# Attention row tiles moved onto multiples of 128, with the last 64 queries of two heads in one tile

## The chip, the cores and the metric

The kernel runs on one core of one Trainium2 chip. The metric is the device time of one execution in microseconds (us), as the median of several runs. A core has TensorE (PE in the profile, its weight loads PEld), VectorE (DVE), ScalarE (ACT), GpSimd (POOL) and SyncE (SP), whose queue issues the DMA transfers.

## What is computed

Three stages follow each other, cut here to what matters:

```
S, D = 576, 64
# 1. causal attention with a cumulative bias, batch 4, 8 heads, head_dim 64
scores = q @ k.T / 8 + min(-(cum[i] - cum[j]), 0)     # masked above the diagonal
x = softmax(scores) @ v
# 2. mixing over the sequence (rank 32), then a feed-forward layer 512 -> 2048 -> 512
u = x + mix(x);  y = u + relu(u @ w_ch1) @ w_ch2
# 3. four attention "experts" (head size 64), each row of y keeps two of four, with gates
out = sum over the two chosen e of w_e * (softmax(q_e @ k_e.T / 8) @ v_e @ wo_e)
```

Both attentions are causal: query row i needs keys 0 to i only. 576 is four times 128 and 64 more.

## The kernel before, in words

**One helper for both attentions.** Class `Attn` serves stage 1 (32 heads, 16 pairs) and stage 3 (16 heads, 8 pairs). A pair is two heads that are worked one after the other; their value products share a PSUM tile. A head's 576 query rows are five row tiles: 64 rows first, then four of 128 that start at 64, 192, 320 and 448. A tile's key width is 64, 192, 320, 448 or 576, since keys beyond the diagonal are left out. A pair is thus ten steps. `run` counts them as `i`, and a step does, in this order of code:

- `qk`: the score products of tile `i` on PE, two matmuls (four for width 576, in two PSUM banks);
- `tr`: the transposes on PE of the tile that is `LAG` steps older (LAG is 10), in blocks of 128 keys, into one of two PSUM tiles `t`. Since tiles end at 64 beyond a multiple of 128, each head also has five tail transposes of 64 keys (line 396) beside its ten of 128 (line 393);
- `peak` (line 363, VectorE): adds the mask, writes the scores to the buffer `P` in SBUF and takes the row maximum;
- `exp` (line 370, ScalarE) of the tile before, in place in `P`, with the row sum;
- `evac` (lines 77 and 79, ScalarE or VectorE as a letter in `ENGA` or `ENGG` says): copies of `t` into the transposed matrix `pt`;
- `norm` (lines 375 to 381), once per head: two small VectorE operations, then GpSimd scales the five tiles of `P`;
- one piece of a value product (`pvq`), then `fillers(i)`.

`P` is two buffers, one for each head of a pair. A tile of `P` is written again ten steps later.

**What fills the steps.** In stage 1 `fillers` takes, per step, pieces of the weight conversion (`convs`: 1 a step, 2 a step between the steps in `FAST`; six pieces convert 128x256 numbers), steps of the operand preparation of the next pair (`PREP`, `PREP1`, `load`), and background work (`BG`: mixing, and the first feed-forward tasks of lines 284 and 298, which wait in the queue until their weight tile is converted). In stage 3 the table `GTAB` names the filler of each step: k and q are query and key products (`g_qk`, line 1064), v values (`g_v`, line 997), a point an output product (`g_out`, line 1087) if one is ready. Stage 2 between them (lines 836 and 854) does not use `Attn`.

**What sets the order.** Stages 1 and 2 run in the order in which the code is written; in stage 3 a scheduler orders each engine's instructions. Each engine works its own queue in order. All DMAs go through SP's queue.

**Operands.** Queries, split into high and low parts, stand in tiles `L1` and `L2`, keys in `R1` and `R2`; the two heads lie side by side. 64 zero columns stand ahead of head 0, so that the first tile can be read as 128 columns. In stage 3 `R1` gets its upper half from `L1` by a DMA, and `L1` then its lower half.

Of the kernel before, what the change touches and what calls it, by code (L numbers as in the profile page):

```python
# [68 lines left out]
TRP = ((1, 0, 2), (2, 2, 3), (3, 3, 4), (4, 0, 0), (0, 4, 5))  # L69
BG = (1, 1, 0, 2, 1)  # L70
# [79 lines left out]
def fused_kernel(ctx, tc, qk, v, s, u, vv, w12, wp, out):  # L150
# [166 lines left out]
    class Attn:  # L317
# [3 lines left out]
        LAG = 10  # L321

        def __init__(self, pools, nq, engines, scale, split=0):
# [4 lines left out]
            self.stat, self.P = [], []  # L328
            for i in range(3):
                t = self.st.tile([P, 3, NT], F32, name=f"stat{i}")  # L330
                nc.vector.memset(t, 1.0)
# [4 lines left out]
            self.pvq = []

        def clear(self, i):


            nc.gpsimd.memset(free_ap(self.pt[i][64:128], 0, [[PST + P, NT], [1, 64]]), 0.0)

        def qk(self, n, t):
            q1, k1, q2, k2 = self.pair_ready(n)
            M, W, i0 = ROWS[t], WID[t], I0[t]
            nb = 1 if W <= 512 else 2
            w = W // nb
            ps = self.psq.tile([P, nb, 512], F32, tag=f"qk{nb}", bufs=1 if nb == 2 else self.nq, name=f"qk_{n}_{t}")
            rows = slice(i0 + M - 64, i0 + M + 64)
            for bk in range(nb):  # L350
                c0 = bk * w
                nc.tensor.matmul(ps[:, bk, :w], lhsT=q1[:, rows], rhs=k1[:, c0:c0 + w], start=True, stop=False)  # L352
                nc.tensor.matmul(ps[:, bk, :w], lhsT=q2[:, rows], rhs=k2[:, c0:c0 + w], start=False, stop=True)  # L353
            return ps[P - M:, :, :w] if nb > 1 else ps[P - M:, 0, :w]
# [11 lines left out]
        def exp(self, n, t):
            M, W = ROWS[t], WID[t]
            stat = self.stat[n % 3]
            po = self.P[n % 2][P - M:, OFF[t]:OFF[t] + W]
            nc.scalar.activation(out=po, in_=po, func=AF.Exp, scale=-1.0, bias=stat[P - M:, 0, t:t + 1],  # L370
                                 accum_out=stat[P - M:, 1, t:t + 1])

        def norm(self, n):
            stat = self.stat[n % 3]
            nc.vector.tensor_scalar(out=stat[:, 2, :], in0=stat[:, 1, :], scalar1=1e-9, scalar2=None, op0=OP.add)
            nc.vector.reciprocal(out=stat[:, 2, :], in_=stat[:, 2, :])  # L376
            gate = self.heads[n].get("gate")
            for t in range(NT):
                r0 = P - ROWS[t]
                pv = self.P[n % 2][r0:, OFF[t]:OFF[t] + WID[t]]  # L380
                nc.gpsimd.tensor_scalar(out=pv, in0=pv, scalar1=stat[r0:, 2, t:t + 1],  # L381
                                        scalar2=1.0 if gate is None else gate(t)[r0:], op0=OP.mult, op1=OP.mult)

        def tr(self, n, r):

            ps = self.pst.tile([P, 512], F32, tag="t", name=f"t_{n}_{r}")
            Pn = self.P[n % 2]
            t, a, e = TRP[r]  # L390
            for kb in range(t):
                c0 = OFF[t] + P * kb
                nc.tensor.transpose(ps[:, P * kb:P * kb + P], Pn[:, c0:c0 + P], ident)  # L393
            for k in range(a, e):
                c0, x = OFF[k] + WID[k] - 64, P * (t + k - a)
                nc.tensor.transpose(ps[0:64, x:x + P], Pn[:, c0:c0 + 64], ident)  # L396
            return ps

        def evac(self, n, r, ps):
            pt = self.pt[n % 3]  # L400
            t, a, e = TRP[r]
            if t:
                cp(nc, self.engines[n % 2][r], free_ap(pt[:, :], I0[t], [[PST, t], [1, P]]), ps[:, :P * t])
            if e > a:
                cp(nc, self.engines[n % 2][r], free_ap(pt[0:64], (PST + P) * a, [[PST + P, e - a], [1, 64]]),
                   free_ap(ps[0:64], P * t + 64, [[P, e - a], [1, 64]]))
# [813 lines left out]
```

## Time and profile before

| what | us |
|---|---|
| median of three runs | 850.0 (849.77 to 850.97) |
| the profiled execution's own time | 849.59 |
| its span, first to last instruction | 847.8 |
| busy in the span | PE 804.4, PEld 743.4, DVE 522.2, ACT 478.3, POOL 329.7 |

The profiled execution stands 1.8 us above its span, and 0.4 us below the median. PE's busy time counts each matmul from its issue to its end; matmuls overlap, so what one costs is read from the distance between the starts of neighbours. The score products of the 24 pairs start at these times: pair 0 at 9.57 us, pair 7 at 115.85, pair 15 (the last of stage 1) at 258.76, pair 16 (the first of stage 3) at 665.45, pair 18 at 699.69, pair 22 at 788.47, pair 23 at 809.74. Stage 2 lies from 295 to 652.

### The profile page before, as it was taken

To read this page: it belongs to the slowest core of one execution; us is meant where nothing else is said; L and a number is where in the kernel's file an instruction comes from. 1 tells how busy PE (TensorE), PEld (TensorE's weight loads), DVE (VectorE), ACT (ScalarE), POOL (GpSimd) and SP (SyncE) were. 2 spreads that over 40 slices of the span, in tenths; PEclk is the share of its full clock that TensorE was granted. 3 is DMA by queue.
4 is the path that set the end of the run, shared out by engine and by line. 5 is a ranking of instruction groups with operands and counts; after the bars stand their busy time and mean duration, and the time that the engine had idled before them with its cause. 6 is when DMAs were issued, how large, how long until landed. Compare 5 with 4: busy or idle time off the path is not lost.

```text
span 847.8 us, 17359 instructions
## 1 busy us (share of the span) xinstructions
PE 804.4 (95%) x6068; PEld 743.4 (88%) x6068; DVE 522.2 (62%) x1547; ACT 478.3 (56%) x1446; POOL 329.7 (39%) x498
## 2 busy tenths in 40 slices
PE   4898799999999999999999999999999989999997
PEld 3676588988888799999999999999999989898875
DVE  7778876786665457646554664464456775656541
ACT  6788777776676445334434443443333576666672
POOL 6656655453453335223422442232333043322241
PEclk9999999999999999999999999999999999999999
DMA  7877566646651151112121221110000221212121
GB/s 212 220 214 208 167 171 187 198 134 169 184 134 44 37 210 51 50 27 55 45 63 26 77 59 42 50 39 26 1 1 2 43 44 29 67 42 54 53 65 62
DMA packets 35897, 75.48 MB, mean 89 GB/s; under 512 B 4584, under 2 KB 8168, under 8 KB 35780
## 3 DMA queue, kind: packets, MB, share of 16 engines
q1 hardware_dynamic: 35812, 74.39, 32.2%
q8 instruction: 48, 0.79, 0.4%
q14 instruction: 37, 0.30, 0.1%
HBM read 38.93 MB, written 8.55 MB: 56 GB/s over the span
## 4 chain that ended last, share of the span: by engine, by line
PE 77%; DVE 5%; ACT 3%; POOL 2%; issue 2%; DMA 0%; SPq 0%; POOLq 0%; DVEq 0%; ACTq 0%
PE hps L836 21%; PE facc L854 21%; PE pv L420 6%; PE qkp L1064 5%; PE t L393 4%; PE facc L298 3%; PE ops L1087 3%; PE hps L284 3%; PE vps L997 3%; PE qk L353 2%; PE qk L352 2%; PE t L396 2%; POOL P L381 2%; DVE P L363 1%; ACT pt L77 1%
## 5 line engine op out<-in xcount | busy, mean ns | idle before, releaser
L268 POOL TENSOR_TENSOR ul<-uT,uh 128x288 fp32r<-128x288 f32 x126 | 101.7, 826 | 172.0 <-ACT uh L267 149.0
L370 ACT ACTIVATE P<-P,stat 64x64 f32<-64x64 f32 (+4 forms) x240 | 133.7, 557 | 44.1 <-DVE stat L363 42.0
L841 DVE SCALAR_TENSOR_TENSOR hl<-hps,hh 128x288 fp32r<-128x288 f32 x110 | 50.4, 458 | 150.0 <-ACT hh L840 150.0
L381 POOL TENSOR_SCALAR P<-P,stat 64x64 f32<-64x64 f32 (+4 forms) x160 | 101.4, 648 | 104.6 <-DVE stat L376 58.1
L363 DVE CUSTOM_DVE_ANT_0 P<-qk,mask 64x64 f32<-64x64 f32 (+4 forms) x240 | 116.4, 487 | 37.6 <-PE qk L353 21.9
L840 ACT ACTIVATE hh<-hps 128x288 fp32r<-128x288 f32 x110 | 45.0, 409 | 147.9 <-PE hps L836 147.6
L77 ACT ACTIVATE pt<-t 64x64 f32<-64x64 f32 (+5 forms) x304 | 89.8, 336 | 41.3 <-PE t L396 35.3
L836 PE MATMUL hps<-uh,wl 128*128 128x288 f32 x376 | 111.2, 296 | 0.0
L836 PE MATMUL hps<-ul,wh 128*128 128x288 f32 x376 | 111.1, 296 | 0.0
L854 PE MATMUL facc<-hh,wh 128*128 128x288 f32 x376 | 111.1, 296 | 0.0
L836 PE MATMUL hps<-uh,wh 128*128 128x288 f32 x376 | 111.0, 295 | 0.0
L854 PE MATMUL facc<-hh,wl 128*128 128x288 f32 x376 | 110.9, 295 | 0.0
L854 PE MATMUL facc<-hl,wh 128*128 128x288 f32 x376 | 110.8, 295 | 0.0
L352 PE MATMUL qk<-R,L 128*128 128x288 f32 (+4 forms) x288 | 94.9, 334 | 16.4 <-DVE L L577 9.6
L393 PE MATMUL t<-ident,P 128*128 128x128 f32 x480 | 88.1, 282 | 11.4 <-ACT pt L77 4.8
L381 POOL TENSOR_SCALAR P<-P,stat,pt 64x64 f32<-64x64 f32 (+4 forms) x80 | 48.5, 620 | 113.1 <-DVE stat L376 57.6
L393 PEld LDWEIGHTS t<-ident,P 128*128 128x128 f32 x480 | 58.8, 142 | 23.3 <-issue 9.4
L352 PEld LDWEIGHTS qk<-R,L 128*128 128x128 f32 x288 | 57.0, 198 | 23.9 <-issue 11.8
L420 PE MATMUL pv<-pt,V 128*64 128x288 f32 (+4 forms) x752 | 76.9, 344 | 0.0
L191 POOL TENSOR_TENSOR wl<-c_a_w,wh 128x256 fp32r<-128x256 f32 x56 | 43.7, 781 | 76.8 <-ACT wh L188 74.2
L836 PEld LDWEIGHTS hps<-uh,wl 128*128 128x128 f32 x376 | 70.9, 189 | 0.0
L854 PEld LDWEIGHTS facc<-hh,wl 128*128 128x128 f32 x376 | 70.9, 188 | 0.0
(186 smaller groups left out, 2145.6 us busy)
## 6 DMA issues: line engine op xcount, KB each, us to landing
c_raw_w<-in_w_dram SPq DMA_DIRECT2D x64, 256.0 KB
uT<-in_qk_dram SPq DMA_DIRECT2D x15, 576.0 KB
L<-HI SPq DMA_DIRECT2D x28, 288.0 KB
V<-in_v_dram SPq DMA_DIRECT2D x16, 320.0 KB
R<-HI SPq DMA_DIRECT2D x14, 288.0 KB
R<-uT SPq DMA_DIRECT2D x14, 288.0 KB
L<-uT SPq DMA_DIRECT2D x14, 288.0 KB
aD<-stage SPq DMA_DIRECT2D x6, 576.0 KB
```

Source lines behind the costliest of these rows:

```text
L77: nc.scalar.activation(out=out, in_=in_, func=AF.Copy)
L268: eng.tensor_tensor(out=l_, in0=src, in1=h_.bitcast(F32), op=OP.subtract)
L352: nc.tensor.matmul(ps[:, bk, :w], lhsT=q1[:, rows], rhs=k1[:, c0:c0 + w], start=True, stop=False)
L363: nc.vector.tensor_tensor_reduce(out=po, in0=view, in1=mk, scale=-self.scale, scalar=3.0e38, op0=OP.add, op1=OP.min, accum_out=stat[P - M: ...
L370: nc.scalar.activation(out=po, in_=po, func=AF.Exp, scale=-1.0, bias=stat[P - M:, 0, t:t + 1], accum_out=stat[P - M:, 1, t:t + 1])
L381: nc.gpsimd.tensor_scalar(out=pv, in0=pv, scalar1=stat[r0:, 2, t:t + 1], scalar2=1.0 if gate is None else gate(t)[r0:], op0=OP.mult, op1=O ...
L393: nc.tensor.transpose(ps[:, P * kb:P * kb + P], Pn[:, c0:c0 + P], ident)
L420: nc.tensor.matmul(out[64 * hh:64 * hh + 64, lo - a:e - a], lhsT=V(hh, kb), rhs=pt[:, PST * kb + lo:PST * kb + e], start=kb == 0, stop=kb ...
L836: nc.tensor.matmul(ps, lhsT=w[:, 0, cs], rhs=x, start=i == 0, stop=i == 11)
L840: nc.scalar.activation(out=hh, in_=ps, func=AF.Relu)
L841: nc.vector.scalar_tensor_tensor(out=hl, in0=ps, scalar=0.0, in1=hh.bitcast(F32), op0=OP.max, op1=OP.subtract)
L854: nc.tensor.matmul(accs[c][d], lhsT=w[:, 1, cs], rhs=x, start=f == fs[0] and i == 0, stop=f == fs[-1] and i == 2)
```

## The change

A head's tiles now start at 0, 128, 256 and 384 with key widths 128, 256, 384 and 512. The last 64 queries of both heads of a pair form a ninth tile of 128 rows and 576 keys. Its scores are a sum: head 0's 64 queries with 64 zero columns behind them, plus 64 zero columns with head 1's 64 queries behind them, eight matmuls into two banks. For that the zeros stand between the heads in `L1` and `L2`, and head 1's queries are rolled by 64 so that its last 64 come first (on the host for stage 1, by split writes and four DMAs in place of two in `g_qk` of stage 3).

A pair is nine steps and `LAG` is 9. `P` is one buffer of nine tiles; a tile is written again nine steps later, in the step in which `tr` reads it. `norm` runs twice a pair, for tiles 0 to 3 at the pair's step 5 and for tiles 4 to 8 at step 1 of the next pair. `tr` of the ninth tile makes five transposes into both PSUM tiles `t`; `evac` makes four copies of them. The mask has a second form for the ninth tile and is built by `Attn`. The gates of stage 3 are placed by a VectorE copy instead of two DMAs. The tables that are counted in steps (`FAST`, `HALVES`, `UFIRST`, `WIDE`, `GTAB`, `BG`, the engines' letters) are written anew.

```diff
-ROWS = [64, 128, 128, 128, 128]
-I0 = [0, 64, 192, 320, 448]
-WID = [64, 192, 320, 448, 576]
+NS = 9
+WID = [128, 256, 384, 512] * 2 + [576]
+OFF = [sum(WID[:s]) for s in range(NS + 1)]
+QB = S + 64
+QA = (0, QB + 64)
-FAST = (40, 70)
+FAST = (36, 63)
-ENGA = ('vaaaaa', 'aavaav')
+ENGA = 'vaaaaavaaavv'
-ENGG = ('aaaava', 'aaaava')
+ENGG = 'aaaaaaaaaavv'
-GTAB = "kkkkvvvvvqqqq......."
+GTAB = "kkkkvvvvvqqqq....."
-BG = (1, 1, 0, 2, 1)
+BG = (2, 1, 1, 0, 2, 1, 1, 1, 1)
...
-        LAG = 10
+        LAG = NS
...
-            for i in range(2):
-                self.P.append(self.st.tile([P, PW], F32, name=f"P{i}"))
-                nc.gpsimd.memset(self.P[i][0:64, 0:64], 0.0)
+            self.P = self.st.tile([P, OFF[NS]], F32, name="P")
...
+        def qk(self, p, s):
+            W = WID[s]
+            if s < NS - 1:
+                h, t = divmod(s, 4)
+                q1, k1, q2, k2 = self.pair_ready(2 * p + h)
+                c0 = QA[h] + P * t
+                ps = self.psq.tile([P, 1, 512], F32, tag="qk1", bufs=self.nq, name=f"qk_{p}_{s}")[:, 0, :W]
+                nc.tensor.matmul(ps, lhsT=q1[:, c0:c0 + P], rhs=k1[:, :W], start=True, stop=False)
+                nc.tensor.matmul(ps, lhsT=q2[:, c0:c0 + P], rhs=k2[:, :W], start=False, stop=True)
+                return ps
+            ps = self.psq.tile([P, 2, 512], F32, tag="qk2", bufs=1, name=f"qk_{p}_{s}")
+            l = [(q[:, 512 + 64 * h:640 + 64 * h], k) for h in range(2)
+                 for q, k in itertools.batched(self.pair_ready(2 * p + h), 2)]
+            for bk in range(2):
+                for x, (q, k) in enumerate(l):
+                    nc.tensor.matmul(ps[:, bk, :HALF], lhsT=q, rhs=k[:, HALF * bk:HALF * bk + HALF],
+                                     start=x == 0, stop=x == 3)
+            return ps[:, :, :HALF]
...
+            for k0 in range(0, WID[s], 512):
+                ps = self.pst.tile([P, 512], F32, tag="t", name=f"t_{p}_{s}_{k0}")
+                for c in range(k0, min(WID[s], k0 + 512), P):
+                    w = min(P, WID[s] - c)
+                    nc.tensor.transpose(ps[0:w, c - k0:c - k0 + P], self.P[:, OFF[s] + c:OFF[s] + c + w], ident)
+                l.append(ps)
...
-                if i % NT == 1 and 1 < i <= n + 1:
-                    self.norm(i // NT - 1)
+                if i % NS == 5 and i < n:
+                    self.norm(i // NS, 0, 4)
+                if i % NS == 1 and 1 < i <= n + 1:
+                    self.norm(i // NS - 1, 4, NS)
...
-            at = 10 * (p - 1)
+            at = NS * (p - 1)
...
             def place():
                 gt = gates[b % 2]
-                nc.sync.dma_start(out=gt[0:64, 1:NT, :], in_=x[64:128, 0:NT - 1, :])
-                nc.sync.dma_start(out=gt[64:128], in_=x[0:64])
+                tt(out=gt, in0=x, in1=wide, op=OP.mult)
+                nc.vector.tensor_copy(out=gt[64:128, NT - 1, 0:E:2], in_=gt[0:64, NT - 1, 1:E:2])
...
             if h == 1 and hf == 1:
                 L1, R1, _ = sets[pr]
-                dma(out=R1[64:128], in_=L1[0:64])
+                dma(out=R1[64:128, 0], in_=L1[0:64, 0])
+                dma(out=R1[64:128, 1, 0:512], in_=L1[0:64, 1, 64:])
+                dma(out=R1[64:128, 1, 512:], in_=L1[0:64, 1, 0:64])
                 dma(out=L1[0:64], in_=L1[64:128])
```

**What moves on PE.** Steps 2 and 3 of pair 7 in stage 1, before (qk_14 is the first head of pair 7, qk_head_tile; t_12 are the transposes of pair 6, mx a mixing task, hps a feed-forward task of twelve matmuls, of which three are shown):

```order
L352 MATMUL qk_14_2_1577<-R1_1_127,L1_1_125 128x320
L353 MATMUL qk_14_2_1577<-HI_1271,L2_1_128 128x320
L393 MATMUL t_12_2_1580<-ident_58,P0_114 128x128 x3
L396 MATMUL t_12_2_1580<-ident_58,P0_114 64x128
L352 MATMUL qk_14_3_1594<-R1_1_127,L1_1_125 128x448
L353 MATMUL qk_14_3_1594<-HI_1271,L2_1_128 128x448
L393 MATMUL t_12_3_1597<-ident_58,P0_114 128x128 x4
L227 MATMUL mx_1_0_0_1606<-ident_58,uT_68 128x128 x4
L284 MATMUL hps_0_2_1615<-uh_0_0_1256,wh_2_1343 128x288
L284 MATMUL hps_0_2_1615<-ul_0_0_1257,wh_2_1343 128x288
L284 MATMUL hps_0_2_1615<-uh_0_0_1256,wl_2_1344 128x288
```

and of the change, with the beginning of step 4 (qk_7_2 is pair 7, step 2; t_6 the transposes of pair 6):

```order
L349 MATMUL qk_7_2_1473<-R1_1_124,L1_1_122 128x384
L350 MATMUL qk_7_2_1473<-HI_1181,L2_1_125 128x384
L396 MATMUL t_6_2_0_1476<-ident_58,P_107 128x128 x3
L222 MATMUL mx_1_0_0_1487<-ident_58,uT_63 128x128 x4
L349 MATMUL qk_7_3_1496<-R1_1_124,L1_1_122 128x512
L350 MATMUL qk_7_3_1496<-HI_1181,L2_1_125 128x512
L396 MATMUL t_6_3_0_1499<-ident_58,P_107 128x128 x4
L349 MATMUL qk_7_4_1510<-R1_1_124,L1_1_122 128x128
L350 MATMUL qk_7_4_1510<-HI_1181,L2_1_125 128x128
L396 MATMUL t_6_4_0_1513<-ident_58,P_107 128x128
```

The products grow from 320 and 448 columns to 384 and 512, the tail transpose (64x128) has gone, and no feed-forward task stands here: its weight tile is now converted later, counted in pairs. In all, 39 feed-forward matmuls left pair 7, and pairs 8 and 9 have 60 each where they had 54 and 27.

**What moves on SP's queue** in the second pair, before (R1, L1, L2 and HI are the low operands of pair 2; uT from in_qk is the load of pair 3):

```order
L682 DMA c_raw_v2_308<-in_vv_dram 128x192
L467 DMA R1_0_121<-uT_68 64x2x576
L467 DMA L1_0_119<-uT_68 64x2x576
L467 DMA L2_0_122<-Cd_142 2x2x576
L467 DMA HI_268<-Cd_142 4x2x576
L524 DMA uT_68<-in_qk_dram 128x2x576
L529 DMA V_1_385<-in_v_dram 128x640
```

and of the change:

```order
L699 DMA c_raw_v2_309<-in_vv_dram 128x192
L535 DMA uT_63<-in_qk_dram 128x2x576
L476 DMA R1_0_118<-uT_63 64x2x576
L476 DMA L1_0_116<-uT_63 64x2x576
L476 DMA L2_0_119<-Cd_139 2x2x576
L476 DMA HI_261<-Cd_139 4x2x576
L540 DMA V_1_366<-in_v_dram 128x640
```

The load of pair 3's raw operands stands ahead of the four moves for pair 2, where it stood behind them.

## Rows read from the trace of the kernel before

**Rows 1.** Windows of seven stretches: length, busy us (x instructions) per engine, PE clock, DMA share, GB/s.

```profile
20.00:62.00 42.00, 36.66 (x261) 29.16 (x261) 31.89 (x112) 34.15 (x118) 25.09 (x39) 1.00 0.85 226
...
62.00:116.00 54.00, 44.28 (x318) 34.06 (x316) 42.67 (x136) 41.95 (x142) 33.59 (x49) 0.97 0.68 185
...
116.00:259.00 143.00, 140.53 (x1128) 125.34 (x1128) 103.98 (x339) 103.80 (x337) 74.14 (x114) 1.00 0.60 160
...
281.00:295.00 14.00, 12.20 (x110) 9.15 (x109) 4.26 (x13) 6.36 (x21) 4.95 (x8) 1.00 0.13 44
...
665.50:699.70 34.20, 31.61 (x237) 29.11 (x235) 27.97 (x112) 25.14 (x79) 9.02 (x15) 1.00 0.18 37
...
699.70:788.50 88.80, 88.63 (x688) 81.42 (x687) 52.33 (x185) 56.92 (x171) 25.78 (x45) 1.00 0.20 52
...
788.50:847.80 59.30, 52.21 (x370) 41.44 (x368) 22.69 (x75) 32.41 (x100) 15.96 (x29) 1.00 0.19 55
```

**Rows 2.** Timeline of PE in five steps of the second attention: start, duration, line, matmul.

```profile
751.10 0.31 PE L352 MATMUL qk<-R,L 128*128 128x320 f32 x1
...
753.41 0.37 PE L352 MATMUL qk<-R,L 128*128 128x448 f32 x1
...
753.83 0.60 PE L393 MATMUL t<-ident,P 128*128 128x128 f32 x4
...
754.40 0.29 PE L1064 MATMUL qkp<-XL,WPh 128*128 128x288 f32 x1
...
755.86 0.29 PE L352 MATMUL qk<-R,L 128*128 128x288 f32 x1
...
756.38 0.28 PE L396 MATMUL t<-ident,P 128*64 128x128 f32 x1
...
756.62 0.28 PE L997 MATMUL vps<-WPl,XH 128*128 128x260 f32 x1
...
757.96 0.19 PE L352 MATMUL qk<-R,L 128*128 128x64 f32 x1
...
759.92 0.25 PE L352 MATMUL qk<-R,L 128*128 128x192 f32 x1
...
761.91 0.31 PE L352 MATMUL qk<-R,L 128*128 128x320 f32 x1
```

**Rows 3.** Lines by form, VectorE: peak of widest and narrowest tile; busy, mean ns.

```profile
L363 DVE CUSTOM_DVE_ANT_0 P<-qk,mask 128x576 f32<-128x576 f32 x48 | 36.1, 753 | 10.1 <-PE t L396 8.4 <-POOL P L381 1.2
...
L363 DVE CUSTOM_DVE_ANT_0 P<-qk,mask 64x64 f32<-64x64 f32 x48 | 10.9, 228 | 7.1 <-PE qk L353 2.7 <-PE t L396 2.3 <-POOL P L381 0.7
```

**Rows 4.** Lines by form, ScalarE: exponential of widest and narrowest tile, small copy.

```profile
L370 ACT ACTIVATE P<-P,stat 128x576 f32<-128x576 f32 x48 | 37.2, 774 | 14.6 <-DVE stat L363 14.6
...
L370 ACT ACTIVATE P<-P,stat 64x64 f32<-64x64 f32 x48 | 16.5, 343 | 7.7 <-DVE stat L363 6.3
...
L77 ACT ACTIVATE pt<-t 64x64 f32<-64x64 f32 x112 | 23.1, 206 | 1.2 <-PE t L396 1.1
```

**Rows 5.** Lines by form, VectorE: the three operations of one weight conversion.

```profile
L113 DVE SCALAR_TENSOR_TENSOR c_s_w<-c_g_w,c_r_w 128x256 uint32<-128x256 uint32 x44 | 27.7, 629 | 1.0 <-ACT c_r_w L110 1.0
...
L121 DVE CUSTOM_DVE_ANT_0 c_a_w<-c_a_w,c_s_w 128x512 uint16<-128x512 uint16 x44 | 22.0, 500 | 1.2
...
L117 DVE TENSOR_SCALAR c_a_w<-c_g_w 128x256 uint32<-128x256 uint32 x44 | 19.6, 445 | 0.0
```

**Rows 6.** Windows of two pairs of the first attention, columns as in the first group.

```profile
115.80:133.30 17.50, 17.09 (x139) 14.76 (x137) 15.29 (x46) 15.97 (x53) 12.35 (x19) 1.00 0.68 170
...
223.10:237.60 14.50, 13.96 (x114) 11.48 (x112) 10.37 (x37) 11.07 (x37) 8.12 (x13) 1.00 0.72 187
```

**Rows 7.** Timeline of SyncE's queue, operand moves at the second attention's start.

```profile
658.98 0.52 SPq L467 DMA_DIRECT2D R<-L  x1
662.13 0.51 SPq L467 DMA_DIRECT2D L<-L  x1
```

**Rows 8.** Line 363, what ended VectorE's idle time before it: us, times.

```profile
  PE t L396: 10.7, 14
```

More of the change, by code (lines that the diff above doesn't have):

```diff
@@ L317, in fused_kernel, with __init__ @@
     class Attn:
[L321 to L323 removed]
+        LAG = NS
+        def __init__(self, pools, nq, engines, scale, split=0, mask=None):
             self.nq, self.scale, self.split = nq, scale, split
@@ L336, in __init__ @@
             self.pvq = []
-        def clear(self, i):
[L341 to L354, printed above, removed]
@@ L366, in exp @@
[L366 to L382, printed above, removed]
@@ L384, in tr @@
[L384 to L406, printed above, removed]
+            self.mask = self.st.tile([P, 800], BF16, name="mask") if mask is None else mask
@@ new lines, in exp, with norm @@
+        def exp(self, p, s):
+            stat = self.stat[p % 2]
+            po = self.P[:, OFF[s]:OFF[s + 1]]
+            nc.scalar.activation(out=po, in_=po, func=AF.Exp, scale=-1.0, bias=stat[:, 0, s:s + 1],
+                                 accum_out=stat[:, 1, s:s + 1])
+        def norm(self, p, a, e):
+            stat = self.stat[p % 2]
+            nc.vector.tensor_scalar(out=stat[:, 2, a:e], in0=stat[:, 1, a:e], scalar1=1e-9, scalar2=None, op0=OP.add)
+            nc.vector.reciprocal(out=stat[:, 2, a:e], in_=stat[:, 2, a:e])
+            for s in range(a, e):
+                h, t = divmod(s, 4) if s < NS - 1 else (0, 4)
+                gate = self.heads[2 * p + h].get("gate")
+                po = self.P[:, OFF[s]:OFF[s + 1]]
+                nc.gpsimd.tensor_scalar(out=po, in0=po, scalar1=stat[:, 2, s:s + 1],
+                                        scalar2=1.0 if gate is None else gate(t), op0=OP.mult, op1=OP.mult)
@@ new lines, in tr, with evac @@
+        def tr(self, p, s):
+            l = []
+            for k0 in range(0, WID[s], 512):
[4 more added lines that the diff above has]
+                l.append(ps)
+            return l
+        def evac(self, p, s, l):
+            if s < NS - 1:
+                h, t = divmod(s, 4)
+                cp(nc, self.engines[s], free_ap(self.pt[(2 * p + h) % 3][:, :], P * t, [[PST, t + 1], [1, P]]),
+                   l[0][:, :WID[s]])
+                return
+            for h in range(2):
+                cp(nc, self.engines[s + h], free_ap(self.pt[(2 * p + h) % 3][:, :], 4 * P, [[PST, 4], [1, 64]]),
+                   free_ap(l[0][:, :], 64 * h, [[P, 4], [1, 64]]))
+            for h in range(2):
+                cp(nc, self.engines[s + 2 + h], self.pt[(2 * p + h) % 3][0:64, PTW - 64:],
+                   l[1][0:64, 64 * h:64 * h + 64])
@@ L609, in pair_ready @@
             h = n % 2
-            L1, L2 = (t[:, S * h:S * h + S + 64] for t in whole[(n // 2) % 2])
+            L1, _, L2 = whole[(n // 2) % 2][:3]
             return L1, R1[:, h, :], L2[0:68], R2[0:68, h, :]
@@ L752, in fillers @@
                     convs.pop(0)()
-            for _ in range(BG[i % NT]):
+            for _ in range(BG[r]):
                 background()
@@ L1172, in _layout @@
     q, k, v, s = (inputs[n] for n in ("q", "k", "v", "s"))
-    qk = np.stack([x.transpose(0, 1, 3, 2).reshape(B, NP, 2, D, S) for x in (k, q)], axis=2)
+    qr = q.copy()
+    qr[:, 1::2] = np.roll(q[:, 1::2], 64, axis=2)
+    qk = np.stack([x.transpose(0, 1, 3, 2).reshape(B, NP, 2, D, S) for x in (k, qr)], axis=2)
     qk = qk.transpose(0, 1, 2, 4, 3, 5).reshape(B, NP, P, 2, S)
```

128 lines of the change are left out of this document (70 added, 58 removed).

## Prediction

> **What bounds the kernel now.** I read the windows first, cut where the work changes, since one busy share over the whole span mixes stages with different limits. Stage 2 holds no attention step and is left alone. In the rest the reader should see three kinds of stretch [rows 1]. From 116 to 259 us and from 699.7 to 788.5 us PE is in flight nearly all the time (140.5 of 143, 88.6 of 88.8 us) while VectorE and ScalarE stand below 75%: 13 pairs (7 to 15, less the end of 15, and 18 to 21) whose length is what PE's stream costs. From 62 to 116 us (pairs 4 to 6) VectorE has 42.7 and ScalarE 42.0 of 54 us, and PE's flight is broken; 665.5 to 699.7 us is like it (VectorE 28.0 of 34.2). There a step passes from engine to engine, with VectorE nearest to a bound. From 20 to 62 us the DMA engines are 85% busy at 226 GB/s, the most of the seven stretches: operand moves set that stretch. The two ends, 281 to 295 and 788.5 to 847.8 us, have few fillers; there the last steps of a pair wait for one copy or exponential after the other.
>
> So a step that is taken away pays where engines wait for each other, and where PE is full only what it saves PE counts.
>
> **PE, pair by pair.** Matmuls overlap, so I price them by the distance of starts [rows 2]. Eleven filler products take 754.40 to 755.86, 0.133 us each, and the value fillers 756.62 to 757.96, 0.122 each. Taking twelve fillers off the five steps (starts at 751.10, 753.41, 755.86, 757.96, 759.92, 761.91) leaves a step's own part: width 320 0.72, 448 0.86, 576 0.64, 64 0.50, 192 0.53 us. That is 3.25 a head and 6.50 a pair. Four transposes and one filler lie between 753.83 and 754.40: 0.11 each. One tail transpose and one filler lie between 756.38 and 756.62: 0.12 for the tail, though it has half the keys. From width 320 to 448, with the same number of transposes, 128 more columns on two products cost 0.14, so 64 cost 0.07; from 64 to 192 they cost 0.03 in all.
>
> The new steps: width 128 is the step of 64 less two tails, plus half of 0.03: 0.27. 256 is that of 192 less a tail, plus 0.045 (between 0.015 and 0.07): 0.46. 384: 0.72 - 0.12 + 0.07 = 0.67. 512: 0.86 + 0.07 = 0.93. The ninth tile has four products and four transposes more than the step of 576: 0.64 + 4 x 0.133 + 4 x 0.11 = 1.61. A pair: 2 x 2.33 + 1.61 = 6.27, so 0.23 less. PE gains little: score columns grow by a sixth, and only the tails pay for it. Over 13 pairs -3.0 us: -2.1 in stage 1, -0.9 in stage 3 (ends -1.3 and -4).
>
> Here a rule speaks against the change. The Trainium skill (TensorE: Matmul & The Clock Gate, LDWEIGHTS (loading the stationary operand)) says that a weight load takes time in proportion to its columns, so a tail with 64 would take half of a full transpose's load. By it the tails that go are worth half, and the sum would be 849.3 instead of 842.5. The trace disagrees: 0.12 us for a tail against 0.11.
>
> **The hole.** A pair has nine conversion pieces instead of ten, so the third feed-forward weight tile is ready a pair later, and 39 matmuls leave pair 7 for pairs 8 and 9. Pair 13, which has no such task before, took 14.5 us, and pair 7 took 17.5 [rows 6]. Pair 7 thus gains at most 3.0, and the 39 cost 39 x 0.133 = 5.2 later: up to +2.2 in all, nothing if pair 7 can run PE-bound without them. I take +1.0. Nine second-step matmuls end up behind the last pair, where PE is not full: nothing.
>
> **62 to 116 us, three pairs.** Peaks: (753 - 228) ns over 512 columns is 1.03 ns a column, 162 ns fixed [rows 3]. Ten tiles with 3200 columns make 4.9 us, nine with 3136 make 4.7: -0.23, and one read of the maximum less, together -0.3. Conversion, two pieces a step here: 18 instead of 20 a pair. Six pieces cost VectorE 0.629 + 0.500 + 0.445 = 1.57 us [rows 5], 0.26 each: -0.5. VectorE's copies stay four a pair. So VectorE saves 0.8 a pair. ScalarE saves more: by the same working 0.84 ns a column and 289 ns fixed, -0.3 for the exponentials, and four copies less of at most 0.206 us [rows 4], in all up to 1.1. The stretch follows the smaller: 3 x 0.8 = -2.5. The conversions are not saved but moved to pairs 13 to 15, under a full PE; without that cover +1.6 comes back. At the other end, if a step's price is fixed, a tenth of the stretch goes: -5.4.
>
> **20 to 62 us.** Bytes set it, and only a conversion piece a pair goes away (a sixth of a 256 KB load, 0.2 us at 226 GB/s). Against that GpSimd now scales four tiles of pair 0 ahead of the second head's split for pair 1, and each pair's operands have five steps, not six, from the last move to the first product, behind the next load in the queue. I take 0; ends -4 (a tenth) and +2.
>
> **Stage 3's start.** The split of one quarter of the query products into two parts gives VectorE two more operations a pair, each at least the 0.228 of the narrowest peak for what little width they take over, and the peaks give 0.3 back: even. The move of the keys' upper half is three issues in front of the one for the lower half, at 0.52 each [rows 7]: up to +1.0 before the first scores at 665.5. Pair 17 loses two steps that have no filler. I take -0.5 (ends -2 and +1.3). Two VectorE operations for the gates in place of one and two DMAs: nothing, beside 28 us.
>
> **The ends.** 281 to 295 us: ten steps become nine, at most a tenth of 14, I take -0.5. 788.5 to 847.8: ScalarE's 1.1 a pair for two pairs, -2.0 (ends 0 and a tenth, -5.9).
>
> **Sum.** 0 - 2.5 - 2.1 + 1.0 - 0.5 - 0.5 - 0.9 - 2.0 = -7.5 us on the profiled execution's 849.6, whose own time lies 0.4 below the median: 842.5 us.
>
> **The new wait.** With one buffer, a tile's peak must come after the transposes that read the same tile in the same step; before, that held for two steps of five, and VectorE already waited 10.7 us in 14 waits for tail transposes [rows 8]. Behind a waiting peak stand VectorE's copies and conversions, and ScalarE's exponential waits for it. Where VectorE is last, PE has run ahead and the transposes are done; where PE is full, VectorE has slack. I price it at nothing in the sum. GpSimd's second `norm` has three steps, not four, before its first transpose; it stands at 62% at most [rows 1].
>
> **The rivals.**
> - *The likeliest* (0.50): as summed, 842.5, by itself 839 to 846.
> - *Steps have a fixed price* (0.20): in the stretches without a full PE (54 + 14 + 34.2 + 59.3 = 161.5 us) handovers set the time. A tenth would be -16; with PE's -2.0 that is 832, and halfway to my sum 837. For it: no engine but PE is over 82% there. Against: the work of a pair stays almost the same.
> - *Tail transposes cost half* (0.06): then each of a pair's eight tails in the shrunken steps saves 0.065 less, a pair comes to 6.79, +0.29, and 13 pairs turn -3.0 into +3.8: 849.3. The rule named above would do this; the one row on a tail speaks against it.
> - *Nothing comes of it* (0.10): copies and peaks were beside other work, and the hole costs 2.2: 849.5.
> - *The same-step wait decides* (0.14), the one on the slower side: 25 transposes in nine steps are 0.31 us a step. If peaks wait for them in the 45 steps of pairs 4 to 6 and 16, 17, that is +14: 856. It turns the sign from 24 such steps on. For it: the 10.7 us. Against: PE's lead there.
>
> **How the numbers follow.** 0.2% of 850 is 1.7 us, about what a measurement of this kernel can tell from no change. Faster (under 848.3): the first two and a little of the fourth, 0.72. Same: most of the third and fourth and the edges, 0.12. Slower: the last and what goes wrong at stage 3's start or in the hole, 0.16. The range reaches below to 834 (a third of the second rival left out) and above to 851.
>
> **What would show it.** Pairs 18 to 21 about 0.2 us shorter each, with 0.11 a transpose; pairs 4 to 6 about 0.8 each; pair 7 without feed-forward matmuls near 14 to 15 us and pairs 8 and 9 longer; from pair 22's start to the end about 2 us less. The prediction is wrong if the peaks' waits for PE grow far beyond 10.7 us in pairs 4 to 6, if pairs 1 to 3 wait for operand moves at their first product, or if the steps of the ends shrink by a tenth.

## The result, and the profile after

The change made the kernel slower: 860.59 us (median of 4 runs, 858.56 to 864.66) against 849.88 on the same chip, a ratio of 1.013 with a 95% interval of 1.0091 to 1.017. The profiled run took 859.64 us, its span is 857.9, 10.1 more than before.

The first view is the windows, cut at the starts of the same pairs as in [rows 1]: pairs 1 to 3, 4 to 6, 7 to 14, 16 and 17, 18 to 21, and from pair 22 to the end. The columns are those of [rows 1].

```profile
21.57:68.97 47.40, 38.77 (x246) 29.59 (x246) 29.30 (x104) 32.64 (x101) 23.27 (x35) 0.86 0.83 206
68.97:120.97 52.00, 44.86 (x304) 34.78 (x302) 40.79 (x126) 38.05 (x119) 31.54 (x43) 0.93 0.70 181
120.97:270.21 149.24, 141.25 (x1078) 123.05 (x1076) 101.42 (x326) 98.48 (x293) 69.83 (x106) 0.99 0.62 157
676.95:714.44 37.49, 34.13 (x256) 31.48 (x256) 28.45 (x114) 24.58 (x73) 11.64 (x18) 1.00 0.15 33
714.44:800.61 86.17, 85.68 (x643) 78.15 (x642) 54.02 (x190) 54.57 (x153) 21.07 (x37) 1.00 0.20 53
800.61:857.90 57.29, 50.24 (x354) 40.68 (x352) 21.32 (x70) 30.52 (x83) 15.22 (x27) 0.98 0.19 57
```

Against the same pairs before, pair 0 is 2.0 us longer (11.8 from first product to first product, 9.8 before), pairs 1 to 3 are 4.6 longer (47.4, 42.8 before), pairs 4 to 6 1.7 shorter (53.7 before), pairs 7 to 14 6.3 longer (142.9 before), 16 and 17 3.3 longer (34.2), 18 to 21 2.6 shorter (88.8) and the end 2.0 shorter (59.3). Two columns have moved with the time: DMA fell from 226 to 206 GB/s in pairs 1 to 3, and PE's granted clock, 1.00 and 0.97 there and in pairs 4 to 6 before, is 0.86 and 0.93.

Three views say where to look. First, what PE waited for from 10 to 62 us (two rows of the view: time in all, number, longest), and the first of them in the kernel before:

```profile
PE qk L349 <- DMA L<-uT: 7.7, 3, 3.4
PE qk L349 <- ACT P L373: 2.5, 1, 2.5
```

```profile
PE qk L352 <- DMA L<-uT: 2.9, 3, 1.4
```

The move into `L` now comes late. SyncE's queue shows what stands ahead of it, here for pair 2:

```profile
28.78 1.21 SPq L535 DMA_DIRECT2D uT<-in_qk_dram  x1
30.04 0.66 SPq L476 DMA_DIRECT2D R<-uT  x1
30.75 0.60 SPq L476 DMA_DIRECT2D L<-uT  x1
31.39 1.39 SPq L476 DMA_DIRECT2D L<-Cd  x1
32.89 0.69 SPq L476 DMA_DIRECT2D HI<-Cd  x1
```

The first row is the raw load of pair 3, the others are pair 2's moves, and pair 2's first product starts at 39.11. In the kernel before, the load stood behind the moves.

Second, what ended VectorE's idle time before a peak, the view of [rows 8]:

```profile
  PE t L396: 48.4, 51
```

Before it was 10.7 us in 14 waits. Of the 48.4 us, 12.2 lie in pairs 1 to 3, 7.3 in pairs 4 to 6, 16.3 in pairs 7 to 14, 0.5 in pairs 16 and 17, 6.5 in 18 to 21 and 5.5 behind them. Third, windows over three stretches in which PE stood still, each with a stretch soon after it:

```profile
35.80:39.00 3.20, 0.00 (x0) 0.00 (x0) 1.40 (x5) 1.68 (x5) 1.40 (x2) 1.00 0.87 179
40.00:42.80 2.80, 2.80 (x12) 1.35 (x10) 0.64 (x4) 0.49 (x2) 0.00 (x0) 0.50 1.04 190
214.70:216.20 1.50, 0.00 (x0) 0.00 (x0) 0.57 (x2) 1.47 (x4) 0.64 (x1) 1.00 0.14 39
217.50:220.50 3.00, 3.00 (x15) 2.43 (x16) 1.39 (x6) 1.01 (x4) 0.00 (x0) 0.50 1.02 226
90.00:91.10 1.10, 0.00 (x0) 0.00 (x0) 0.67 (x2) 1.10 (x4) 1.10 (x3) 1.00 0.91 127
95.00:101.00 6.00, 6.00 (x28) 4.31 (x27) 3.31 (x11) 2.93 (x9) 3.63 (x6) 0.50 0.50 132
```

Where PE does nothing the clock column still says 1.00; soon after, PE works at 0.50, the lower of its two levels (1.2 GHz).

### The profile page after: what moved, and what is told of

It reads as the page before. It is cut to its first block, busy times and chain, and to the rows that moved or that the text cites. A ratio compares the mean times of both kernels' runs of the same rounds, so it can differ in the third digit from the quotient of the medians.

```text
span 857.9 us, 16751 instructions
## 1 busy us (share of the span) xinstructions
PE 805.7 (94%) x5948; PEld 740.8 (86%) x5948; DVE 515.6 (60%) x1517; ACT 461.4 (54%) x1310; POOL 319.3 (37%) x476
## 4 chain that ended last, share of the span: by engine, by line
PE 77%; DVE 9%; ACT 4%; POOL 3%; DMA 3%; issue 3%; SPq 0%; POOLq 0%; ACTq 0%; DVEq 0%
PE hps L853 20%; PE facc L871 20%; PE pv L425 8%; PE t L396 5%; PE qkp L1080 4%; PE ops L1107 3%; PE facc L293 3%; DVE P L367 3%; DMA L<-uT 3%; PE qk L349 2%; PE vps L1014 2%; PE hps L279 2%; PE qk L350 2%; PE qk L357 2%; POOL P L384 2%
## 5 line engine op out<-in xcount | busy, mean ns | idle before, releaser
L373 ACT ACTIVATE P<-P,stat 128x128 f32<-128x128 f32 (+4 forms) x216 | 126.0, 584 | 49.0 <-DVE stat L367 48.0
L384 POOL TENSOR_SCALAR P<-P,stat 128x128 f32<-128x128 f32 (+2 forms) x144 | 93.1, 663 | 123.4 <-DVE stat L379 105.2
L396 PE MATMUL t<-ident,P 128*128 128x128 f32 x600 | 105.5, 282 | 10.3 <-ACT pt L77 5.4
L77 ACT ACTIVATE pt<-t 128x256 f32<-128x256 f32 (+2 forms) x208 | 86.0, 427 | 51.9 <-PE t L396 50.1
L396 PEld LDWEIGHTS t<-ident,P 128*128 128x128 f32 x600 | 75.2, 143 | 27.5 <-issue 12.1
L349 PE MATMUL qk<-R,L 128*128 128x128 f32 x192 | 70.6, 368 | 24.2 <-DVE L L592 9.8
L384 POOL TENSOR_SCALAR P<-P,stat,pt 128x128 f32<-128x128 f32 (+4 forms) x72 | 45.7, 649 | 118.2 <-DVE stat L379 57.4
L425 PE MATMUL pv<-pt,V 128*64 128x288 f32 (+4 forms) x752 | 80.6, 351 | 1.9 <-DVE stat L367 1.9
L367 DVE CUSTOM_DVE_ANT_0 P<-qk,mask 128x128 f32<-128x128 f32 (+3 forms) x128 | 61.7, 484 | 23.8 <-PE t L396 20.2
L425 PEld LDWEIGHTS pv<-pt,V 128*64 128x64 f32 x752 | 51.8, 140 | 26.6 <-issue 6.4
```

What stands on the lines that cost most here:

```text
L77: nc.scalar.activation(out=out, in_=in_, func=AF.Copy)
L349: nc.tensor.matmul(ps, lhsT=q1[:, c0:c0 + P], rhs=k1[:, :W], start=True, stop=False)
L384: nc.gpsimd.tensor_scalar(out=po, in0=po, scalar1=stat[:, 2, s:s + 1], scalar2=1.0 if gate is None else gate(t), op0=OP.mult, op1=OP.mult)
L396: nc.tensor.transpose(ps[0:w, c - k0:c - k0 + P], self.P[:, OFF[s] + c:OFF[s] + c + w], ident)
L425: nc.tensor.matmul(out[64 * hh:64 * hh + 64, lo - a:e - a], lhsT=V(hh, kb), rhs=pt[:, PST * kb + lo:PST * kb + e], start=kb == 0, stop=kb ...
```

## The experiments

The theories: **1**, the operand moves come late (a step less of lead, and behind the next raw load). **2**, with one P buffer a step's peak must wait for the transposes of the same step. **3**, the feed-forward work pushed out of pair 7 costs. The expectations call 2 and 3 rivals too. Ratios are to the kernel before, on the same chip, with the 95% interval.

| run | median us | ratio |
|---|---|---|
| e1 load behind the moves | 855.91 | 1.0039 (1.0010 to 1.0067) |
| e2 moves one step earlier | 857.21 | 1.0063 (1.0045 to 1.0081) |
| e3 second head first | 861.05 | 1.0093 (1.0056 to 1.0130) |
| e4 lag 8 in both attentions | 856.41 | 1.0049 (1.0029 to 1.0068) |
| e5 e1 and lag 8 in stage 3 | 849.29 | 0.9975 (0.9954 to 0.9996) |
| e6 e1 and more conversions | 857.90 | 1.0080 (1.0050 to 1.0111) |
| e7 e1 and transposes first | 851.39 | 0.9993 (0.9974 to 1.0011) |
| e8 kernel before, moves late | 855.75 | 1.0053 (1.0032 to 1.0074) |
| e9 three repairs | 848.14 | 0.9974 (0.9960 to 0.9989) |
| e10 e9 without e1's edit | 854.37 | 1.0044 (1.0029 to 1.0060) |
| e11 e9 and two edits at the start | 850.74 | 1.0004 (0.9992 to 1.0017) |
| e12 idle time filled | 862.34 | 1.0115 (1.0087 to 1.0144) |

**e1 and e2, the moves.**

```
-LOAD = -6                       # e1
+LOAD = -5
-PREP = (-1, 0, 1, 2, 4)         # e2, in place of e1's edit
+PREP = (-1, 0, 1, 2, 3)
```

> The changed kernel (860.6 us) with one number altered: the load of a pair's raw operands is issued one step later, so that it again stands behind the four moves of the pair before it in SP's queue. Theory 1 (late operand moves: the raw load of 590 KB stands ahead of the moves in a stretch where the DMA engines are over 80% busy): the waits of the first score products for the move into L at 25.6 and 35.7 us (2.26 and 3.39 us) shrink by about 2 us each, pair 2 starts near 36 us in place of 39.1, and the time is 855 to 857. Rival 2 (the step's wait on the one P buffer is what costs): pair 2 may start earlier, but the sum over pairs 3 to 14 stays, 858 to 861. Rival 3 (the FFN work that was pushed from pair 7 into pairs 9 to 13): no change in pairs 7 to 14, same bound as rival 2.

> The changed kernel with the four moves of a pair from pair 2 on issued at step 3 in place of step 4 of the pair before: six steps ahead of the first product as in the kernel before, and ahead of the raw load of the same step. Theory 1: at least what the load behind the moves gives, 853 to 857, with the waits for the move into L gone from pair 2 on (3.39 and 1.7 us in the changed kernel) and TensorE's granted clock in 21 to 53 us higher than 0.71 and 0.88. Rivals 2 and 3: 858 to 861, the waits for P and the FFN spread as they are.

Both times came as theory 1 had them, e2 0.2 us above its range; the waits for the move into `L` shrank less than it said (5.4 us are left in e1, 2.2 in e2). In e1's queue the load follows the moves:

```profile
29.53 0.78 SPq L476 DMA_DIRECT2D R<-uT  x1
30.37 0.60 SPq L476 DMA_DIRECT2D L<-uT  x1
31.02 0.82 SPq L476 DMA_DIRECT2D L<-Cd  x1
31.96 0.75 SPq L476 DMA_DIRECT2D HI<-Cd  x1
32.75 0.59 SPq L535 DMA_DIRECT2D uT<-in_qk_dram  x1
```

The last move is issued 0.9 us sooner than in the changed kernel, yet pair 2's first product starts 2.5 sooner (36.58). So the earlier issue alone does not explain it. The rest fits the bytes of the load, which no longer go ahead: 576 KB are 2.6 us at the 226 GB/s of [rows 1]. No row shows the landing of a single move. The Trainium skill has a rule on this order (DMA: Bandwidth & Descriptors, Queues, rings and completion order): on each DMA engine the descriptors of a queue are consumed in the order of their ring. The 2.5 us agree with it. The waits for the move into `L` fell from 7.7 to 5.4 us, and the one of 1.7 at pair 12 is gone. In e2 pair 3 starts at 48.95 (51.16 in e1, 53.04 in the changed kernel, 46.20 before), but its pair 5 ran at a clock of 0.77 and took 22.4 us.

**e8, the same harm done to the kernel before.**

```
-PREP = (-1, 0, 1, 2, 4)
+PREP = (-1, 0, 1, 2, 5)
```

> The kernel before (850 us) with the four operand moves of a pair from pair 2 on issued a step later, at step 5 of ten: five steps ahead of the first product and behind the raw load of the next pair, as the change has them. Theory 1: pair 2 starts 2 to 3 us later, waits for the move into L appear at the first products of pairs 2 and later in the DMA-bound stretch, and the time is 853 to 855. Rivals 2 and 3: no change, 849 to 851.

The time rose by 0.5%, just above theory 1's figure: pair 2 starts at 36.81 (33.13 before), behind a new wait:

```profile
PE qk L352 <- DMA V<-in_v_dram: 4.7, 1, 4.7
```

The view names the last transfer of those that the product stood behind. Nothing but the moves' place changed, in a kernel of ten steps and two P buffers.

**e3, the start.**

```
-PREP1 = (0, 3, 3, 5, 5, 5, 7, 7)
+PREP1 = (0, 3, 3, 4, 4, 5, 7, 7)
```

> The changed kernel with pair 1's second head split on GpSimd at step 4, ahead of the first normalization (step 5), in place of step 5 behind it; the moves of its first head also go a step earlier. Theory 1's second part: the moves of the second head are issued near 17.3 us in place of 20.0, the wait of 2.26 us at 25.6 us goes, and the time falls by 2 to 3 us to about 858. Rivals 2 and 3: pair 1 shortens but the next waits, for the moves of pair 2, take it back: 860 to 861.

As the rivals had it: pair 1 is shorter by 1.1 us, starts 0.9 later, and pair 2 starts at 38.91, 0.2 sooner.

**e4 and e5, one step less between scores and transposes.**

```
-        LAG = NS                # e4
+        LAG = NS - 1
+        attn.LAG = NS - 1       # e5: e1's edit, and this for stage 3 alone
```

> The changed kernel with the transposes eight steps behind the scores in place of nine, so that a tile of P is read out one step before its slot is written again; nothing of the operand moves is altered. Theory 1: no gain, 859 to 862, as the first 30 us stay as they are; the rows of DVE's peak waiting for PE's transposes fall all the same. Rival 2 (the same-step wait, 9.8 us of DVE's peaks waiting for transposes in 62 to 137 us): the waits go and pairs 4 to 7 and 13 fall by about 1 us each, 854 to 857. Slower than the changed kernel if the normalization on GpSimd, with one step less ahead of the transposes, becomes what they wait for.

> The kernel of e1 (load behind the moves, 855.9 us) with the transposes eight steps behind the scores in stage 3 alone. Theory 2 (in stage 3 the wait of a step's peak for the transposes of the same step sets pairs 16 to 18): pair 17 falls from 20.2 to about 17.0 us as in e4, pair 22's start comes 2 to 3 us sooner against pair 15's, and the time is 852 to 854. Theory 1 alone (only operand moves of stage 1 cost): no change, 855 to 857.

e4 gave theory 2's figure, but not as it said: in its trace pair 16 starts 2.7 us later than in the changed kernel (679.67), and the whole gain is in stage 3. e5 did better than expected. Stage 3, pairs 16 and 17, 18 to 21, 22 to the end, in e5:

```profile
668.73:703.16 34.43, 32.92 (x248) 30.08 (x247) 27.75 (x114) 24.92 (x72) 10.15 (x16) 1.00 0.16 36
703.16:789.98 86.82, 86.27 (x652) 79.07 (x651) 53.37 (x190) 56.43 (x154) 23.13 (x39) 1.00 0.19 51
789.98:845.40 55.42, 49.94 (x353) 39.26 (x351) 21.20 (x70) 30.00 (x82) 15.27 (x27) 0.99 0.20 62
```

176.7 us in all, 181.0 in the changed kernel, 182.4 before. Other runs repeat this: from pair 16's start to the end e1, e2, e3, e6 and e12, with lag 9, take 180.8 to 181.1 us, and e4, e9, e10 and e11, with lag 8, 176.5 to 177.1. Most of the gain is in the steps without fillers. Here are the first four and the last five steps of pair 17, windows of the changed kernel and of e5:

```profile
694.31:703.02 8.71, 8.71 (x69) 8.55 (x67) 7.24 (x33) 5.21 (x16) 3.21 (x5) 1.00 0.08 19
703.02:714.44 11.42, 9.13 (x71) 7.16 (x70) 6.26 (x24) 7.39 (x24) 5.25 (x9) 1.00 0.19 41
```

```profile
686.14:694.95 8.81, 8.81 (x69) 8.64 (x67) 7.75 (x35) 6.75 (x19) 3.22 (x5) 1.00 0.08 19
694.95:703.16 8.21, 7.79 (x62) 5.64 (x60) 5.00 (x21) 6.22 (x21) 3.74 (x7) 1.00 0.26 55
```

With twelve fillers in each step the lag makes no difference; the five steps without are 3.2 us shorter. Not all of that is waiting: e5 has nine matmuls fewer in these five steps and nine more in pairs 18 to 21, which are 0.7 us longer. Nor does the wait of theory 2 show there: the peaks of these steps wait 0.5 us for transposes in the changed kernel. PE itself waits 1.0 us for a peak's maxima, 0.8 for a copy on ScalarE and 0.5 for the write of `L` there, and 0.3 in all in e5. How the lag shortens the chain between them is not shown.

The rest of e5's lead over e1 is luck with the clock. Its stage 1 is that of e1, yet in the traces pair 5 took 2.9 us less. The rows are pair 5 of e1 and of e5:

```profile
82.09:102.27 20.18, 17.35 (x106) 13.01 (x104) 12.74 (x42) 13.66 (x42) 10.70 (x15) 0.83 0.64 165
```

```profile
81.07:98.34 17.27, 14.44 (x106) 10.99 (x104) 13.01 (x42) 13.66 (x42) 10.59 (x15) 1.00 0.76 198
```

The same 106 matmuls, at a mean clock of 0.83 and at 1.00. A clock of 0.83 over 20.18 us is 6.9 us at half speed (an estimate), which cost 2.9. All ten runs of each say the same: e1's three runs with a mean clock of 0.996 or more took 850.7 to 851.0 us, its seven others, at 0.990 or less, 855.4 to 860.0. e5's two runs at 0.997 took 846.4 and 846.6. At equal clock e5 is thus some 4.4 us faster, about what lag 8 gives stage 3 (the two chips differ by 0.5 us in the kernel before); the rest of the 6.6 us between the medians goes with how often the clock fell.

**e6, the hole in pair 7.**

```
 LOAD = -5
-FAST = (36, 63)
+FAST = (26, 63)
```

> The kernel of e1 with two weight pieces a step from step 27 on in place of step 37, ten more before pair 7, so that the third feed-forward weight tile is ready as early as in the kernel before. Rival 3 (the feed-forward work pushed out of pair 7 costs): pair 7 has its 39 feed-forward matmuls again, pairs 9 to 13 fall by 3 to 5 us in sum and the time is 851 to 853. Theory 1: pairs 3 and 4, where two pieces a step now stand, and the DMA engines are over 70% busy, take back what pairs 7 to 13 give: 855 to 857.

Theory 1's reading came true, and worse. Pair 7 has 30 feed-forward matmuls again, and pairs 7 to 14 take 144.1 us (second row), 145.6 in e1; but pairs 3 to 6 take 76.4 (first row, at a clock of 0.87), 69.0 in e1 (at 0.93):

```profile
49.67:126.10 76.43, 64.39 (x408) 50.18 (x405) 52.40 (x167) 52.91 (x162) 43.27 (x60) 0.87 0.68 181
126.10:270.24 144.14, 138.56 (x1078) 122.15 (x1076) 98.90 (x322) 96.71 (x287) 67.71 (x103) 1.00 0.60 159
```

**e7, transposes ahead of the scores.**

```
-                view = self.qk(*divmod(i, NS)) if i < n else None
                 ps = self.tr(*divmod(j, NS)) if 0 <= j < n else None
+                view = self.qk(*divmod(i, NS)) if i < n else None
```

> The kernel of e1 with the transposes of a step issued ahead of the score products of the step on TensorE. The same-step wait (theory 2) is then behind the transposes anyway, so DVE's peaks wait for score products and the row of peaks waiting for transposes, 14.9 us in 62 to 155 us in e1, falls to near nothing. If what costs is the order (a peak waits for transposes issued behind its own scores), 852 to 854; if the transposes only take the same time in front of the scores, 855 to 857; slower, 858 or more, if the transposes wait for GpSimd's scaling and hold the scores up.

A little faster than the first reading; this trace is of e7's fastest run. Peaks now wait nearly as long for PE, but for scores:

```profile
  PE qk L350: 22.7, 38
  PE qk L357: 15.4, 14
  PE t L396: 7.1, 6
```

So the sum of these waits is no price: 45.2 us here and, counted in the same way, 52.9 in the changed kernel (48.4 for transposes, 4.5 for scores) and 32.6 in the kernel before, whose time e7 has. In stage 1, pairs 3 to 6 took 65.6 us and pairs 7 to 14 145.0; in e5, with the same clock (0.97 and 1.00), 66.2 and 145.7. The order is worth about 1.3 us there, by one trace of each; stage 3 takes 179.2 us, 1.7 less than in the changed kernel.

**e9, e10 and e11, put together.** e9 has e1's edit, e7's order in stage 1 and lag 8 in stage 3; e10 is e9 with `LOAD = -6`; e11 is e9 with e3's edit, and with the second write of the decay rows (`Cn[:, 0:2, 0:64]`) moved from ahead of the loop to its step 6.

> The changed kernel with the three repairs that the earlier runs point to: the raw load behind the moves (e1), the transposes ahead of the step's scores in stage 1 (as e7), the transposes eight steps behind in stage 3 (as e5). If they add up: stage 1 as in e7 (pair 15 starts near 260 us, 1 us after the kernel before), stage 3 and its end as in e5 (176.7 us from pair 16's start to the end, 182.4 before), so 845 to 847 us, 0.4 to 0.6% under the kernel before. If the gain of e7 and that of e5 were one and the same (the clock staying up), 849 to 851.

> As e9 without the first repair: the raw load again ahead of the moves. Theory 1 (the order of the moves costs by itself): the waits for the move into L stay at 7 us or more in 20 to 62 us, pair 2 starts near 39 us, and the time is 3 to 5 us above e9, 849 to 852. Rival 2 (only the step's wait costs, and the late moves are hidden once it is gone): within 1.5 us of e9.

> As e9, and at the start the second write of the decay rows, one issue of 0.6 us on SP's queue, goes behind the moves of pair 1's first head, and pair 1's second head is split on GpSimd at step 4, ahead of the first normalization. Theory 1 (pairs 0 and 1 are late for two more reasons: two more issues on SP ahead of pair 1's load and moves, and GpSimd's scaling of four tiles ahead of the second head's split): pair 1 starts near 20.5 us in place of 21.7, pair 2 near 34.5 in place of 36.3, and the time is 1 to 2 us under e9, 843.5 to 846. Rival: the DMA engines set pairs 1 and 2, and pair 2 starts no sooner: as e9.

e9 beats both kernels, by 0.26% under the one before, though it ends 1 us above its range. e10 is 6.2 us above e9, more than expected: late moves cost by themselves, with the step's chain mended. Part of that price comes by way of the clock: in the traces 2.5 of 4.7 us lie in pair 5, at 0.74 in e10 and 0.90 in e9. e11 failed. Pair 1 starts 2.6 us sooner than in e9 and then takes 19.3 us in place of 14.1 (first row pair 0, second pair 1):

```profile
9.72:19.73 10.01, 7.17 (x25) 6.28 (x26) 8.67 (x26) 6.73 (x21) 3.83 (x7) 1.00 0.57 147
19.73:39.03 19.30, 11.97 (x64) 9.15 (x62) 10.77 (x37) 11.59 (x36) 7.88 (x12) 0.82 0.91 216
```

**e12, the clock.**

```
+WARM = {8: 20, 12: 20, 17: 32, 107: 16}
             for _ in range(BG[r]):
                 background()
+            if i in WARM:
+                ps = psq.tile([P, 1, 512], F32, tag="qk1", name=f"warm_{i}", bufs=4)[:, 0, :]
+                for _ in range(WARM[i]):
+                    nc.tensor.transpose(ps[:, :P], ident, ident)
```

> The changed kernel (860.6 us) as it is, its waits included, with 88 extra transposes of the identity on TensorE that nothing reads, put where TensorE waits for operand moves: 20 at the end of pair 0, 20 after step 3 of pair 1, 32 at the end of pair 1, 16 at the end of pair 11, 0.1 us each. In the changed kernel the granted clock falls to half a microsecond or so after each of these four waits (0.50 from 22.9 to 32.8, from 39.9 to 42.9 and from 217.4 to 220.6 us). If the half clock behind the waits is a cost of its own: the clock of pairs 1, 2 and 12 (0.71, 0.88, 0.91) goes up to 0.95 or more, pairs 1 and 2 and 12 fall by 4 to 7 us in sum, and the time is 854 to 857. If the stretch is set by the DMA engines whatever TensorE's clock, or if the transposes only lengthen the waits: the clock rises and the time stays, 860 to 863.

The second reading came true for the time, but the trace is mixed. Windows of pairs 1, 2, 3, 7 and 12, and of pair 12 in the changed kernel:

```profile
22.80:39.75 16.95, 14.55 (x117) 12.85 (x115) 9.08 (x34) 10.45 (x35) 7.40 (x11) 1.00 0.94 222
39.75:52.40 12.65, 11.10 (x81) 8.43 (x82) 8.03 (x30) 8.26 (x26) 7.57 (x11) 1.00 0.83 205
52.40:71.34 18.94, 17.25 (x107) 13.03 (x104) 10.74 (x37) 12.71 (x39) 8.00 (x12) 0.82 0.65 166
124.04:143.25 19.21, 17.48 (x107) 13.13 (x105) 10.76 (x36) 12.68 (x40) 10.02 (x15) 0.82 0.66 156
222.29:238.95 16.66, 16.66 (x137) 15.00 (x135) 10.60 (x35) 9.54 (x29) 6.79 (x11) 1.00 0.65 161
```

```profile
216.29:234.78 18.49, 18.37 (x133) 16.22 (x134) 10.57 (x35) 9.43 (x28) 6.77 (x11) 0.91 0.58 147
```

The clock of pairs 1, 2 and 12 is 1.00. One trace does not show that the transposes did it: e6, which up to pair 2 is the kernel of e1, has 1.00 in pairs 1 and 2, where e1 has 0.89 and 0.88. Pairs 1 and 2, with the DMA engines 94 and 83% busy, became only 0.6 and 1.3 us shorter; pair 12, where PE is full, 1.8. Pairs 3 and 7 now have a low clock that they did not have in the changed kernel, and are 3.0 us longer each; in e3, without the extra transposes, pair 7 has 0.82 as well.

## Why the prediction was wrong, point by point

**20 to 62 us, priced at nothing (ends -4 and +2).** This is the step that failed. I named the two facts, five steps in place of six and the load ahead of the moves, in the stretch that I had called bound by operand moves, and still wrote 0. The changed kernel reached pair 3 6.8 us later than the one before. The moves' share is shown from both sides: e1 gives back 4.4 us by pair 15's start, e10 against e9 6.2 us, and e8 costs the kernel before 4.1 us (855.75 against 851.68 on that chip). Part of it lies far from this stretch: the wait of 1.7 us at pair 12, and the 1.8 us that the half clock behind it costs (pair 12 is 16.7 us in e1 and e12, which have neither). The sign that I had set for this came true: pair 1 waits 2.0 us for a move at its first product and 2.3 at that of its second head, pair 2 3.4 at its first.

**The new wait, priced at nothing; the rival at +14.** This is the second term that failed. My mark for it was waits far beyond 10.7 us in pairs 4 to 6. They came over the whole kernel, 48.4 us; pairs 4 to 6 have 7.3 (0.2 before), and the 45 steps that the rival counted 7.8. Most of these waits cost nothing, as e7's 45.2 show. The price is in stage 3, 4.3 us (181.0 to 176.7) against my 0, and about 1.3 in stage 1. Where most of the gain lies, in the five steps of pair 17, the rival's mechanism does not show: peaks wait 0.5 us for transposes there. That a step less of lag removes it is shown; how much of it is the P buffer and how much the copies was not separated.

**Pairs 7 to 14, with the hole (+1.0).** The largest miss: I had -2.1 and +1.0, and they are 6.3 longer. 3.6 went with e1 (149.2 to 145.6), among it the wait and the clock of pair 12. The hole is right in kind and too small: pair 7 without its feed-forward work fell by 1.3 us (17.4 to 16.2), not by up to 3.0, and e6, which puts most of that work back, takes pairs 7 to 14 down by 1.5. I had also taken PE to be full there. It stands still 2.5 of 142.9 us before, but 8.0 in the changed kernel and 6.4 in e1, there mostly in pairs 7, 10 and 13 (1.9, 1.8 and 2.0 us). Why is open.

**PE, step by step.** Right where PE has work in every step. With 1.60 us for twelve fillers taken off, the changed kernel's four steps of pair 17 are 0.29, 0.46, 0.66 and 0.90 us, by their starts:

```profile
694.31 0.22 PE L349 MATMUL qk<-R,L 128*128 128x128 f32 x1
...
696.20 0.28 PE L349 MATMUL qk<-R,L 128*128 128x256 f32 x1
...
698.26 0.33 PE L349 MATMUL qk<-R,L 128*128 128x384 f32 x1
...
700.52 0.39 PE L349 MATMUL qk<-R,L 128*128 128x512 f32 x1
...
703.02 0.22 PE L349 MATMUL qk<-R,L 128*128 128x128 f32 x1
```

I had 0.27, 0.46, 0.67 and 0.93, with a tail at the price of a full transpose. The ninth step, at 1.61 in the prediction, took 1.52 in pair 19 (753.91 to 755.43, no filler). The rival in which tails cost half is out: by it these steps would be longer by 0.065 for each tail that went. That is what the Trainium skill's rule would have made (TensorE: Matmul & The Clock Gate, LDWEIGHTS (loading the stationary operand)); the trace disagrees here too, and before, a tail's weight load took 112 ns on average, a full transpose's 142.

**Pairs 4 to 6, -2.5.** Measured -1.7 with a clock of 0.83 in pair 5, and -3.5 in e5 (50.2 us). **The ends.** From pair 22 on -2.0, as predicted, but by luck: lag 8 takes another 1.9 off there (57.3 to 55.4), so the gain was larger and the wait that I had priced at nothing hid half of it. The drain of stage 1 gave nothing (pair 15 and stage 2 together +0.05). **Pairs 18 to 21, -0.9.** They are 2.6 shorter, but with 643 matmuls in place of 688 [rows 1], and only 20 of the 45 are transposes that the change removes: work lies in other pairs, and only the whole can be judged. From pair 16 to the end I had -3.4; the changed kernel has -1.4, e5 -5.7. Pairs 16 and 17, at -0.5 in the prediction, are 0.2 longer than before in e5 and 3.3 longer in the changed kernel.

**What was in no term: the clock.** Behind many of PE's waits its clock dropped, and in these traces a drop went with 1.8 to 3.0 us in a pair that is not bound by DMA (pair 12, 5, 3, 7), and with 0.6 and 1.3 in pairs 1 and 2, where the DMA engines are 94 and 83% busy. In pairs 3 to 7 it comes and goes between runs of the same stage 1. The Trainium skill has it for waits for DMA (TensorE: Matmul & The Clock Gate, HAM oscillation — how this bites in real kernels): such a wait lets the clock be throttled, and the next tile starts slow. The rows of 35.8 and 214.7 us show this order: 3.2 and 1.5 us without a matmul, then work at 0.50.

**Still open.** Pair 13 takes 15.8 us or more in all kernels of nine steps, 14.5 before [rows 6]; none of the runs shortened it. And pair 3 starts 2.8 to 6.0 us late even with the repairs (e2, e9); of its two suspects, SyncE's extra issues and GpSimd's scaling ahead of the second head's split, e11 treated both at once and only moved the wait.

With e5's repairs the span is 2.4 us under that of before: the change gains 5.7 us in stage 3, and stage 1 takes 3.3 of it back.

## What to carry to other kernels

When a loop gets fewer steps, every table written in steps shrinks in time: ask of each prefetch how long its lead is now, and whether an event that stood behind another at the same step now stands ahead of it in the queue. Price a lost lead in a stretch bound by DMA by the bytes that get in front, never at nothing. A sum of waits is no price: look where the waiting engine has no other work, and compare those steps between runs that differ in one edit. When one kernel's runs spread over several us, as e1's do from 850.7 to 860.0, compare runs of equal granted clock before crediting an edit.

## What was unexpected in the hardware

The granted clock fell behind short waits, and not each time. In the changed kernel 1.66 us without a matmul ahead of 216.29 were followed by 3 us at 0.50. In pair 5 PE waits four times, for 0.51, 1.19, 0.20 and 0.93 us, before the same matmuls in the changed kernel, in e1 and in e5. In the changed kernel 6 us at 0.50 follow (95 to 101 us) and in e1 the pair's clock is 0.83; in e5 it stays at 1.00. So the fall of a pair's clock in one trace shows neither that an edit caused it nor, when it is absent, that an edit cured it.
